# Turning the local probabilities of 26 of 32 head pairs on VectorE instead of TensorE

## The chip, the cores and the metric

The kernel runs on one core of a Trainium2 chip. The metric is device time in microseconds. The kernel before took 578.76 us, the median of three runs (578.58 to 580.44).

A core has five engines that each work through an instruction list of their own, in order: TensorE (PE in the profile; its weight loads are PEld), VectorE (DVE), ScalarE (ACT), GpSimd (POOL) and SyncE (SP, which here issues nearly all DMAs). They wait for each other through semaphores.

## The reference

For 8 batches, 8 heads, a sequence of 576 and a head size of 64, the output of an attention with two resolutions goes through a gated MLP:

```python
# per batch and head
out_d   = softmax(scale * q_d @ k_d.T) @ v_d      # q, k, v averaged over 4 positions: 144 x 144
mask    = abs(i - j) < 4                          # 7 diagonals of the 576 x 576 scores
out_loc = softmax(where(mask, scale * q @ k.T, -1e9)) @ v
x = repeat(out_d, 4) + out_loc                    # heads side by side: 576 x 512 per batch
# per batch
h = gelu_tanh(x @ w_in);  u, v = halves of h      # 512 -> 1024
v_n = layernorm(v) * g;   v_s = w_sg @ v_n + b_sg # mixes the 576 positions
y = x + (u * v_s) @ w_out
```

All of it is float32. The matrix products of the MLP are made of three products of a high and a low part each, which is why they fill most of TensorE's time.

## The kernel before

**Pairs.** Two heads make a pair of 128 partitions, and pairs are numbered 0 to 31 (`g`), four per batch. The local attention never builds the 576 x 576 scores. The queries are cut into ten blocks of 58 (`QB`), and the keys that a block can see lie in a window of 64 (`KB`), so a pair's local scores are ten tiles of 64 queries by 64 keys for each of two heads. The tile `ms` holds them as 128 partitions x 10 x 64: partitions 0 to 63 are queries of one head, 64 to 127 of the other. Within a window, query j sees keys j to j+6, so all else in the 64 x 64 tile is zero after the exponential.

**Steps of a pair,** by the names of its tasks: `lq lk lv lw` load; `qs ks vs` pool over four positions; `YS` makes both kinds of scores on TensorE; `ma mb` add the mask (L463); `mx nx my ny` find the maxima; `ea eb ec` take exponentials on ScalarE (L515, L523); `re rc` sums and reciprocals; `np` (L537) normalises the local probabilities in `ms`, on GpSimd or VectorE; `nq` (L540) the pooled ones. Then both are turned, since the product with `v` needs keys on the partitions: `T` (four transposes through TensorE, L543, each 122 queries x 128 keys, into a PSUM bank), `U` (a fifth of these, and three of the pooled ones, L552) and `t` (two pooled). `pa` and `pb` copy the local results from PSUM into a buffer `pt` (helper `copy`, L232), on ScalarE or VectorE; `pc pe` do so for the pooled ones. `D` (L604, L620) multiplies with `v` on TensorE, and `oe od xa xb xh xl xc` merge, store in `x` and split it into a high and low part.

**MLP of a batch:** `v u s o` on TensorE (L722 and L800) and, between them, work on the other engines: `vg vb vp vn vh vl ua sa sm gh gl oa os`.

**Order.** Every engine's list follows one text, `ORDER`, that names all tasks, with the engine behind a slash where it isn't the first that the task allows (`np23/V`: VectorE). It was written by a planner beforehand; at build time `place()` only walks it. So where a task stands in `ORDER` decides what stands in front of it and behind it on its engine. The dictionaries in `add(...)`, such as `{"A": 0.52, "V": 0.58}`, are the planner's costs in us, and have no effect on what is built.

**Buffers.** `place()` also hands out buffers, first freed first used: 8 PSUM banks (`ps`), 10 large buffers (`X`) and 38 of `R`. A task that takes a buffer waits for the last readers of what was in it. `ms` is an `X`; `pt`, `pdt`, the loaded `q k v` and most of the MLP's operands are `R`.

Of the kernel before, what the change touches and what calls it, by code (L numbers as in the profile page):

```python
# [112 lines left out]
YS9 lq11 nq8/P od7 xa7 xb7 xh7/A T8 ma9 my9 mb9 mx9 ny9/A ec9 U8 nx9/V ea9 t8 pa8/V pb8/V qs11/V ks10/V xl6/P pc8/A
pe8/V xl7/P os0.0 v1.0 vg1.0 vb1.0 v1.1 vg1.1 lv8 vs8 D8 oe8/A od8 YS10 my10 eb9 xa8 xb8 xc6 lv9 xc7 vb1.1 ma10 re9/V
v1.4 va1.4/A mb10 xh8/A vs9 vp1.1 vn1.1 v1.3 rc9 nq9/V lk12 vg1.3 v1.2 vp1.0 np9/P t9 T9 vj1.4 vn1.0 U9 o0.2 vg1.4 lw9
lk11 vg1.2 ks12/P pa9/A pb9/A pc9/A lq12 ks11/P ny10/A mx10 nx10/A ec10 vb1.3 vp1.3 vn1.3 vh1.3/A vl1.3/P pe9/V
vh1.1/V u1.2 vb1.2 vp1.2 ea10 oa0.2 oa0.3 D9 YS11 vb1.4 my11 vh1.0/V vl1.0/P eb10 ny11/V ma11 mb11 oe9/V re10/A u1.1
rc10 np10/V vl1.1/V nq10/P ec11 u1.4 ua1.4 ua1.2 u1.0 ua1.0 os0.3 vp1.4 ua1.1 mx11 vn1.2 vh1.2/V vl1.2/P T10 pa10/A
vn1.4 lv10 vh1.4/A vl1.4/V vs10 t10 U10 pb10/V u1.3 ua1.3 pc10/V pe10/A lq13 nx11/A ea11 s1.3 qs12/V eb11 xl8/V od9
xa9 s1.0 s1.1 sa1.1 sa1.0 sm1.1/V lk13 re11/A rc11 lw10 D10 YS12 oe10/A lv11 vs11 xb9 sa1.3 xh9/A np11/P sm1.0/P  # L120
nq11/P u1.6 lw11 lq14 qs13/P my12 ny12/A ma12 s1.2 mb12 mx12 ec12 nx12/V ea12 od10 xa10 s1.5 eb12 sa1.2 ua1.6 s1.4
xl9/P T11 xc8 os0.2 pa11/A sm1.3/V sm1.2/P gh1.1/A re12/V rc12 t11 np12/V sa1.5 nq12/P sa1.4 U11 pb11/V pc11/V u1.5
xb10 pe11/A ua1.5 sm1.5/P ks13/V t12 D11 YS13 lv12 oe11/A od11 xa11 lk15 xb11 ma13 T12 pa12/A U12 pb12/A xh10/A s1.6
mb13 pc12/V pe12/A my13 ny13/V ec13 mx13 nx13/V s1.7 lk14 ks14/V u1.7 xl10/V xh11/V xl11/V sm1.4/P v2.0 u2.6 ks15/P
eb13 vs12 qs14/P sa1.6 ea13 re13/V ua2.6 rc13 ua1.7 vg2.0 v2.3 os0.1 np13/P T13 pa13/A gh1.0/V gl1.0/P lw12 sm1.6/V
D12 lv13 oe12/A sa1.7 sm1.7/V gh1.3/V gl1.3/V gl1.1/V YS14 nq13/P U13 od12 xa12 gh1.2/A lw13 t13 vg2.3 vb2.0 xc11 ma14
mb14 gl1.2/P lq15 o1.4 my14 pb13/V xb12 ny14/V vs13 mx14 v2.1 ec14 lq16 o1.0 pc13/V nx14/A vp2.0 vn2.0 vh2.0/V pe13/V
D13 oa1.4 ea14 qs15/V eb14 oa1.0 YS15 my15 re14/V ny15/V ec15 ma15 mb15 mx15 rc14 v2.2 vg2.2 lk16 xc10 xc9 v2.4 lv14
vg2.1 vs14 np14/V vb2.1 T14 lw14 va2.4/A vj2.4 nx15/A nq14/P vl2.0/V oe13/A od13 xa13 xb13 ks16/P vp2.1 qs16/V vn2.1
vh2.1/A pa14/A lq17 U14 pb14/V t14 vg2.4 pc14/A pe14/A o1.5 u2.0 oa1.5 os1.2 ua2.0 u2.4 ua2.4 vb2.2 vp2.2 vn2.2  # L130
vh2.2/V xh13/A o1.2 ea15 D14 vb2.4 oe14/A vl2.2/P eb15 vp2.4 re15/A YS16 ma16 u2.1 oa1.2 mb16 o1.6 mx16 nx16/V o1.7
lq18 o1.3 eb16 lk18 vb2.3 my16 vl2.1/P ny16/V vn2.4 vh2.4/A oa1.6 xh12/A ec16 vp2.3 vn2.3 vh2.3/V vl2.3/V vl2.4/P
# [879 lines left out]
```

## Time and profile before

| | |
|---|---|
| runs | 578.76 us median (578.58 to 580.44) |
| profiled execution, span | 578.3 us |
| TensorE busy | 562.3 us, 97% |
| TensorE weight loads busy | 524.0 us, 91% |
| VectorE busy | 420.8 us, 73% |
| ScalarE busy | 355.8 us, 62% |
| GpSimd busy | 309.6 us, 54% |
| mean granted TensorE clock | 0.991 |

The span runs from the first to the last instruction of one profiled execution; it lies 0.5 us under the median of the runs. A busy share is that of the whole span. TensorE's matmuls are pipelined, so the duration of one is longer than the distance to the next; where a cost of TensorE is needed, distances from start to start are read. VectorE's instructions can overlap a little with the next one too. In the profile's rows a group reads: line, engine, operation, output<-inputs, form, count | busy us in total, mean ns of one | idle time of the engine before them, and what ended it.

### The profile page before, as it was taken

Reading aid. Unit: us, or ns where it says so; the run is one execution under the profiler, and the core shown is the slowest. Engines: PE = TensorE matmul, PEld = TensorE weight load, DVE = VectorE, ACT = ScalarE, POOL = GpSimd, SP = SyncE. Lnnn points to the kernel's source line nnn. Section 1 sums busy time; section 2 is a strip of 40 time slices with the busy share of each in tenths; the row PEclk is TensorE's granted clock in tenths of the full one; section 3 lists DMA queues with packets and bytes.
Section 4 is the critical chain, followed back from the end, with each engine's and each line's share of the span. In section 5 each row is a group of like instructions: output and inputs, shape, how many; then the busy total and the mean of one; then the engine's idle time right before and its main releaser. Section 6 shows DMA issues by size and latency. Waiting matters only on the chain.

```text
span 578.3 us, 17588 instructions
## 1 busy us (share of the span) xinstructions
PE 562.3 (97%) x7040; PEld 524.0 (91%) x7040; DVE 420.8 (73%) x943; ACT 355.8 (62%) x1239; POOL 309.6 (54%) x391
## 2 busy tenths in 40 slices
PE   7986999999999999999999999999999999999997
PEld 5775899989998899979999899988999889998997
DVE  7987989878877886677567678878757687553552
ACT  4895996978775794475648596465825678211310
POOL 6685647776875546524567824375266743401330
PEclk9897999999999999999999999999999999999999
DMA  8879214263435031610216413143326330001102
GB/s 310 276 234 313 98 45 120 96 192 87 140 96 164 24 107 54 208 63 1 86 56 197 114 67 98 41 151 98 87 83 195 103 107 2 18 23 41 43 1 102
DMA packets 30609, 62.73 MB, mean 108 GB/s; under 512 B 3648, under 2 KB 3904, under 8 KB 30528
## 3 DMA queue, kind: packets, MB, share of 16 engines
q1 hardware_dynamic: 29952, 60.39, 33.1%
q8 instruction: 55, 0.90, 0.7%
q10 hardware_dynamic: 576, 1.23, 0.6%
q14 instruction: 26, 0.21, 0.1%
HBM read 52.17 MB, written 9.44 MB: 107 GB/s over the span
## 4 chain that ended last, share of the span: by engine, by line
PE 91%; DVE 4%; DMA 2%; ACT 2%; issue 1%; ACTq 0%; DVEq 0%
PE ps L800 55%; PE ps L722 18%; PE ps L604 4%; PE ps L620 3%; PE ps L455 3%; PE ps L543 3%; PE ps L476 3%; PE ps L552 2%; DMA R<-in_qT_dram 1%; PE ps L955 1%; ACT L523 1%; ACT pd L523 1%; DVE stats L485 0%; PE ps L448 0%; DMA R<-in_v_dram 0%
## 5 line engine op out<-in xcount | busy, mean ns | idle before, releaser
L800 PE MATMUL ps<-wsg_h,R 128*128 128x288 f32 x576 | 120.5, 296 | 0.0
L800 PE MATMUL ps<-X,weight_z 128*128 128x288 f32 x512 | 109.4, 297 | 0.0
L800 PE MATMUL ps<-R,weight_r 128*128 128x288 f32 x768 | 108.4, 297 | 1.0 <-ACT R L734 0.8
L800 PEld LDWEIGHTS ps<-R,weight_r 128*128 128x128 f32 x768 | 103.1, 188 | 2.2 <-ACT R L734 0.9
L722 PE MATMUL ps<-weight_y,X 128*128 128x512 f32 x320 | 99.1, 404 | 0.0
L515 ACT ACTIVATE X<-X,nb 128x64 f32<-128x64 f32 x280 | 93.6, 339 | 2.8 <-DVE nb L494 2.3
L800 PEld LDWEIGHTS ps<-wsg_h,R 128*128 128x128 f32 x576 | 94.0, 188 | 0.2 <-DVE R L791 0.2
L800 PE MATMUL ps<-wsg_l,R 128*128 128x288 f32 x320 | 92.5, 295 | 0.0
L800 PEld LDWEIGHTS ps<-X,weight_z 128*128 128x128 f32 x512 | 84.3, 188 | 0.5
L800 PE MATMUL ps<-R,weight_z 128*128 128x288 f32 x256 | 75.5, 295 | 0.0
L722 PEld LDWEIGHTS ps<-weight_y,X 128*128 128x128 f32 x320 | 59.4, 191 | 12.5
L838 DVE SCALAR_TENSOR_TENSOR vs<-ps,g_sb,b_sb 128x288 f32<-128x288 f32 x64 | 32.7, 514 | 49.3 <-PE ps L800 43.9
L232 ACT CAST R<-R 128x512 fp32r<-128x512 f32 (+2 forms) x41 | 26.0, 645 | 62.4 <-DVE R L845 35.2
L800 PEld LDWEIGHTS ps<-wsg_l,R 128*128 128x128 f32 x320 | 60.3, 188 | 0.0
L763 POOL TENSOR_TENSOR rs<-rs,nhalf 128x1 f32<-128x1 f32 (+1 forms) x40 | 25.5, 641 | 64.9 <-DVE rs L754 60.9
L515 ACT ACTIVATION_READ_ACCUMULATOR X<-X,nb 128x1 f32 x280 | 53.5, 191 | 0.0
L722 PE MATMUL ps<-weight_y,R 128*128 128x512 f32 x128 | 51.2, 400 | 0.0
L439 POOL TENSOR_TENSOR pairs<-R 112x256 f32<-112x256 f32 x56 | 44.4, 793 | 9.2 <-DMA R<-in_v_dram 9.2
L845 POOL TENSOR_TENSOR R<-R,vs 128x288 f32<-128x288 f32 x27 | 23.7, 880 | 47.1 <-DVE vs L838 32.0
L800 PEld LDWEIGHTS ps<-R,weight_z 128*128 128x128 f32 x256 | 48.2, 188 | 0.2
L232 ACT COPY R<-ps 112x288 f32<-112x288 f32 (+4 forms) x77 | 30.1, 419 | 27.5 <-PE ps L543 20.0
L791 POOL TENSOR_TENSOR R<-R,R 128x512 fp32r<-128x512 f32 (+1 forms) x22 | 30.6, 1393 | 28.4 <-DVE R L232 6.4
(124 smaller groups left out, 1197.3 us busy)
## 6 DMA issues: line engine op xcount, KB each, us to landing
R<-in_v_dram SPq DMA_DIRECT2D x56, 224.0 KB, 3.8
X<-in_vw_dram SPq DMA_DIRECT2D x31, 320.0 KB, 4.2
R<-in_kT_dram SPq DMA_DIRECT2D x31, 293.0 KB, 4.3
out_dram<-R SPq DMA_DIRECT2D x31, 288.0 KB, 3.0
R<-in_qT_dram SPq DMA_DIRECT2D x30, 293.0 KB, 4.0
weight_y<-in_w_in_dram SPq DMA_DIRECT2D x4, 512.0 KB, 6.0
weight_z<-in_w_in_dram SPq DMA_DIRECT2D x4, 512.0 KB, 6.1
weight_r<-in_w_out_dram SPq DMA_DIRECT2D x4, 512.0 KB, 6.6
```

What stands on the lines that cost most here:

```text
L232: (nc.scalar.copy if e == "A" else ENG[e].tensor_copy)(**kw)
L439: ENG[e].tensor_tensor(out=pairs, in0=v[:, 0:2], in1=v[:, 2:4], op=ALU.add)
L455: nc.tensor.matmul(out=sp[i][os, c * KB:(c + 1) * KB], lhsT=q[hs, t * QB:t * QB + KB], rhs=k[hs, t * QB:t * QB + KB], start=not early, sto ...
L476: nc.tensor.matmul(out=st["sdv"][n][os, cs], lhsT=qd2[par][hs, i * QC:i * QC + HD], rhs=st["kd"][hs, ks], start=True, stop=True)
L515: nc.scalar.activation(out=st["ms"][:, t, :], in_=src, func=AF.Exp, bias=st["nb"][:, t:t + 1], scale=scale, accum_out=sums[par][:, t:t + 1])
L604: nc.tensor.matmul(out=out, lhsT=lhsT, rhs=pdt[ks, probs, h * QC:(h + 1) * QC], start=first, stop=last)
L722: nc.tensor.matmul(out=acc, lhsT=r32(l), rhs=r32(weights[f"y{k}"][:, 0, w]), start=(i == 0 and ks[0] == 0), stop=(i == len(ops) - 1 and ks ...
L763: nc.gpsimd.tensor_tensor(out=rs[0:n], in0=rs[0:n], in1=nhalf[0:n], op=ALU.pow)
L791: ENG[e].tensor_tensor(out=r32(dst), in0=vact[s][0][0:n], in1=vh[0:n, 0:DM], op=ALU.subtract)
L800: nc.tensor.matmul(out=acc[:, 0:HALF], lhsT=r32(l), rhs=r32(r), start=(first and n == 0), stop=(last and n == len(ops) - 1))
L838: nc.vector.scalar_tensor_tensor(out=vsb[i], in0=at["ps", "m", b, "s", i][:, 0:HALF], scalar=g_sb[:, i // 2:i // 2 + 1], in1=b_sb[:, half( ...
L845: ENG[e].tensor_tensor(out=u[:, half(i)], in0=u[:, half(i)], in1=vsb[i], op=ALU.mult)
```

## The change

From pair 6 on (`FLIP = 6`), the local probabilities don't pass through TensorE. Twelve VectorE instructions per pair write them turned, straight from `ms` into one of two kept buffers `pz` (pool `Z`), which are zeroed once on GpSimd (`hz0`, `hz1`). Each instruction turns a strip of five 32 x 32 squares (32 partitions x 160 elements in, the same out), one square from each of five of the ten tiles. Of the four squares of a 64 x 64 tile the one with queries 32 to 63 and keys 0 to 31 is always zero and is left alone, so three squares for each of two heads (`a`) and two tile parities (`i`) make twelve.

`T`, `pa` and `pb` are gone for these pairs, and `U` keeps only its three pooled transposes. The four tasks `h{g}.0` to `h{g}.3`, three instructions each, stand in `ORDER` where `T{g}` stood. `R` shrinks from 38 to 35 buffers. A few loads (`lq17 lk17 lq18 lk18 lk24 lq28 lv30`) stand later, `os2.0` and two high parts (`vh5.1 vh5.3`) moved by a few places; else the order is as before.

```diff
+SQ = 32
...
-SIZES = {"ps": 8, "X": 10, "R": 38}
+SIZES = {"ps": 8, "X": 10, "R": 35, "Z": 2}
+FLIP = 6
...
+    pz = [const.tile([P, NTP, 2, KB], F32, name=f"pz{i}") for i in range(SIZES["Z"])]
...
+    for i, t in enumerate(pz):
+        add(f"hz{i}", {"P": 0.6}, lambda e, t=t: nc.gpsimd.memset(t, 0.0))
...
+        def flips(a, i):
+            def emit(e):
+                st["pt"] = pz[where["Z", "pt", g]]
+                src = st["ms"].rearrange("p (c i) k -> p c i k", i=2)[:, :, i]
+                for qb, kb in ((0, 0), (0, 1), (1, 1)):
+                    qs, ks, k0 = a * KB + qb * SQ, slice(kb * SQ, (kb + 1) * SQ), i * KB + kb * SQ
+                    nc.vector.transpose(out=st["pt"][k0:k0 + SQ, :, a, qb * SQ:(qb + 1) * SQ], in_=src[qs:qs + SQ, :, ks])
+            return emit
...
         def turn2(e):
             t2 = buf("ps", "t", g, 2)
-            turn_pair(t2[:, 0:LD], 4)
+            if not flip:
+                turn_pair(t2[:, 0:LD], 4)
...
-            v, pt = st["vw"], st["pt"].rearrange("p c (a q) -> p c a q", a=2)
+            v, pt = st["vw"], st["pt"] if flip else st["pt"].rearrange("p c (a q) -> p c a q", a=2)
...
-                                         rhs=pt[ks, c, h ^ int(2 * c + i >= NA)], start=True, stop=True)
+                                         rhs=pt[ks, c, h ^ int(2 * c + i >= NA), 0:QB], start=True, stop=True)
...
+        if flip:
+            flipped = [f"h{g}.{i}" for i in range(4)]
+            for n, (a, i) in enumerate(((0, 0), (0, 1), (1, 0), (1, 1))):
+                add(flipped[n], {"V": 0.7}, flips(a, i), [N("np")] + (flipped[:1] if n else []),
+                    takes=[] if n else [("Z", "pt", g)], gives=[("X", "ms", g)])
+        else:
+            flipped = [N("pa"), N("pb")]
...
         add(N("D"), {"T": 2.8 if early_d else 1.0}, av,
-            [N("pa"), N("pb"), N("lw"), N("pc"), N("pe"), N("D", 2), N("lv" if early_d else "vs")],
+            flipped + [N("lw"), N("pc"), N("pe"), N("D", 2), N("lv" if early_d else "vs")],
```

An excerpt of `ORDER` around pair 23, before and after:

```diff
-re23/A rc23 nq23/V ks24/V np23/V vg4.3 vb4.3 o3.5 oa3.5 u4.6 ua4.6 ua4.4 ua4.3 vl4.0/P lw22 D22 vp4.3 vn4.3 lw23
-oe22/V YS24 oa3.0 oa3.1 lq26 vh4.3/V T23 pa23/A u4.5 ua4.5 ma24 mb24 mx24 nx24/V eb24 vh4.4/V vl4.4/V vl4.3/P s4.0
+re23/A rc23 nq23/V np23/V o3.5 lk24 ks24/V vg4.3
+vb4.3 oa3.5 u4.6 ua4.6 ua4.4 ua4.3 vl4.0/P lw22 D22 vp4.3 vn4.3 lw23 oe22/V YS24 oa3.0 oa3.1 lq26 vh4.3/V h23.0
+h23.1 h23.2 h23.3 u4.5 ua4.5 ma24 mb24 mx24 nx24/V eb24 vh4.4/V vl4.4/V vl4.3/P s4.0
```

More of the change, by code (lines that the diff above doesn't have):

```diff
@@ L113 @@
[L113 to L132, printed above, removed]
@@ new lines @@
+re8/A o0.4 ks9/V oa0.4 xc5 t7 np7/P h7.0 h7.1 h7.2 h7.3 oa0.0 oa0.5 vs7 U7 pc7/A xc4 rc8 oa0.1 np8/P o0.3 pe7/V D7
+oe7/V xh6/A YS9 lq11 nq8/P od7 xa7 xb7 xh7/A h8.0 h8.1 h8.2 h8.3 ma9 my9 mb9 mx9 ny9/A ec9 U8 nx9/V ea9 t8 qs11/V
+ks10/V xl6/P pc8/A pe8/V xl7/P os0.0 v1.0 vg1.0 vb1.0 v1.1 vg1.1 lv8 vs8 D8 oe8/A od8 YS10 my10 eb9 xa8 xb8 xc6 lv9
+xc7 vb1.1 ma10 re9/V v1.4 va1.4/A mb10 xh8/A vs9 vp1.1 vn1.1 v1.3 rc9 nq9/V lk12 vg1.3 v1.2 vp1.0 np9/P t9 h9.0 h9.1
+h9.2 h9.3 vj1.4 vn1.0 U9 o0.2 vg1.4 lw9 lk11 vg1.2 ks12/P pc9/A lq12 ks11/P ny10/A mx10 nx10/A ec10 vb1.3 vp1.3 vn1.3
@@ new lines @@
+vh1.3/A vl1.3/P pe9/V vh1.1/V u1.2 vb1.2 vp1.2 ea10 oa0.2 oa0.3 D9 YS11 vb1.4 my11 vh1.0/V vl1.0/P eb10 ny11/V ma11
+mb11 oe9/V re10/A u1.1 rc10 np10/V vl1.1/V nq10/P ec11 u1.4 ua1.4 ua1.2 u1.0 ua1.0 os0.3 vp1.4 ua1.1 mx11 vn1.2
+vh1.2/V vl1.2/P h10.0 h10.1 h10.2 h10.3 vn1.4 lv10 vh1.4/A vl1.4/V vs10 t10 U10 u1.3 ua1.3 pc10/V pe10/A lq13 nx11/A
+ea11 s1.3 qs12/V eb11 xl8/V od9 xa9 s1.0 s1.1 sa1.1 sa1.0 sm1.1/V lk13 re11/A rc11 lw10 D10 YS12 oe10/A lv11 vs11 xb9
+sa1.3 xh9/A np11/P sm1.0/P nq11/P u1.6 lw11 lq14 qs13/P my12 ny12/A ma12 s1.2 mb12 mx12 ec12 nx12/V ea12 od10 xa10
@@ new lines @@
+u2.1 oa1.2 mb16 o1.6 mx16 nx16/V o1.7 o1.3 eb16 vb2.3 my16 vl2.1/P ny16/V vn2.4 vh2.4/A oa1.6 xh12/A ec16 vp2.3 vn2.3
+vh2.3/V vl2.3/V lk18 vl2.4/P ua2.1 s2.4 lw15 od14 xa14 oa1.7 oa1.3 o1.1 lq18 lq17 xl13/V qs18/P lk17 xb14 u2.2 s2.0
+sa2.0 rc15 oa1.1 s2.2 nq15/V s2.1 ea16 np15/V s2.3 sa2.1 u2.3 xl12/P lv15 re16/A vs15 sm2.0/V sa2.2 sm2.1/P s2.6 h15.0
+h15.1 h15.2 h15.3 ua2.2 rc16 nq16/P np16/V h16.0 h16.1 h16.2 h16.3 gh2.0/A gl2.0/P xc13 ks17/V U15 os1.0 t15 sa2.3
+ua2.3 sm2.3/V sm2.2/V sa2.4 s2.5 gh2.1/A xh14/V gl2.1/P sm2.4/P qs17/P u2.5 sa2.5 u2.7 pc15/V pe15/A ua2.5 sa2.6
@@ new lines @@
+np21/V vg4.2 v4.4 va4.4/A U20 h21.0 h21.1 h21.2 h21.3 vb4.2 vg4.1 vb4.1 h20.0 h20.1 h20.2 h20.3 vj4.4 t20 pc20/V
+pe20/A lk23 ks23/V v4.0 vg4.0 D20 vp4.2 oe20/V YS22 ma22 mb22 t21 U21 pc21/V pe21/A mx22 lv21 my22 ny22/V ec22 nx22/A
+qs23/P ea22 vb4.0 u4.2 od20 xa20 xb20 eb22 re22/A o3.2 oa3.2 vs21 lq24 D21 lv22 YS23 ma23 mb23 my23 mx23 vp4.1 vn4.1
+vh4.1/A vs22 lk25 ny23/V ec23 vn4.2 oe21/V od21 xa21 rc22 u4.3 nq22/P nx23/V u4.0 ua4.0 o3.0 ua4.2 qs24/V u4.1 t22
+vh4.2/A np22/V h22.0 h22.1 h22.2 h22.3 U22 ua4.1 vl4.2/P os2.3 pc22/A pe22/A vp4.0 vn4.0 v4.3 xb21 vg4.4 vb4.4 ks25/V
@@ new lines @@
+xh21/V vp4.4 vl4.1/P eb23 u4.4 vh4.0/V vn4.4 o3.3 oa3.3 o3.1 ea23 re23/A rc23 nq23/V np23/V o3.5 lk24 ks24/V vg4.3
+vb4.3 oa3.5 u4.6 ua4.6 ua4.4 ua4.3 vl4.0/P lw22 D22 vp4.3 vn4.3 lw23 oe22/V YS24 oa3.0 oa3.1 lq26 vh4.3/V h23.0 h23.1
+h23.2 h23.3 u4.5 ua4.5 ma24 mb24 mx24 nx24/V eb24 vh4.4/V vl4.4/V vl4.3/P s4.0 sa4.0 sm4.0/V lv23 s4.2 lw24 vs23
+xl21/V ea24 s4.1 qs26/V sa4.2 sa4.1 sm4.1/P s4.3 my24 ny24/V sa4.3 U23 ec24 t23 s4.5 u4.7 sm4.2/P sm4.3/V gh4.0/V
+gh4.1/V gl4.1/V gl4.0/V lq25 xh20/A od22 qs25/V re24/A rc24 nq24/P np24/V xa22 sa4.5 pc23/V pe23/A sm4.5/P xb22 s4.4
@@ new lines @@
+ec26 u5.0 u5.4 vn5.2 v5.3 vg5.3 xb24 vs25 pe25/V ua5.0 vn5.1 xh24/A vh5.2/V D25 lv26 vs26 YS27 ma27 lq29 vp5.0 mb27
+oe25/A my27 u5.2 ua5.2 ua5.4 mx27 lw27 qs29/P o4.1 vl5.2/P ny27/A vn5.0 vh5.0/A os2.0 vl5.0/P eb26 u5.5 od25 xa25 xb25
+vb5.3 vp5.3 vn5.3 o4.0 oa4.0 vb5.4 vp5.4 vn5.4 o4.5 ea26 re26/V ec27 o4.3 oa4.3 o4.4 lq28 vh5.1/A vh5.3/A lk29 u5.3
+rc26 nx27/A vl5.1/V eb27 lk28 vh5.4/V vl5.3/V vl5.4/V s5.5 s5.0 nq26/V sa5.0 sm5.0/P np26/V s5.2 s5.1 sa5.2 sm5.2/P
+xl24/P ea27 lw26 re27/A qs28/P u5.1 oa4.4 ua5.3 s5.3 ua5.1 oa4.5 os4.3 sa5.1 s5.4 oa4.1 sm5.1/V sa5.3 xh25/A rc27
@@ L681, in attention @@
         add(N("nq"), {"P": 0.98, "V": 0.5}, norm_d, [N("rc")])
-        add(N("T"), {"T": 0.44}, turn, [N("np")], takes=[("ps", "t", g, 1)], gives=[("X", "ms", g)])
-        add(N("U"), {"T": 0.42}, turn2, [N("np"), N("nq")], takes=[("ps", "t", g, 2)], gives=[("X", "ms", g)])
+        if flip:
[5 more added lines that the diff above has]
+            flipped = [N("pa"), N("pb")]
+            add(N("T"), {"T": 0.44}, turn, [N("np")], takes=[("ps", "t", g, 1)], gives=[("X", "ms", g)])
+            add(N("pa"), {"A": 0.52, "V": 0.58}, evac(0, 4, 1), [N("T")], takes=[("R", "pt", g)], gives=[("ps", "t", g, 1)])
+            add(N("pb"), {"A": 0.18, "V": 0.19}, evac(4, 1, 2), [N("U"), N("pa")])
@@ L684, in attention @@
+        add(N("U"), {"T": 0.42}, turn2, ([] if flip else [N("np")]) + [N("nq")], takes=[("ps", "t", g, 2)],
+            gives=[] if flip else [("X", "ms", g)])
         add(N("t"), {"T": 0.31}, turn3, [N("nq")], takes=[("ps", "t", g, 3)])
-        add(N("pa"), {"A": 0.52, "V": 0.58}, evac(0, 4, 1), [N("T")], takes=[("R", "pt", g)], gives=[("ps", "t", g, 1)])
-        add(N("pb"), {"A": 0.18, "V": 0.19}, evac(4, 1, 2), [N("U"), N("pa")])
-        add(N("pc"), {"A": 0.35, "V": 0.44}, evac_d(0, 3, 2, LD), [N("U"), N("pb")], takes=[("R", "pdt", g)], gives=[("ps", "t", g, 2)])
+        add(N("pc"), {"A": 0.35, "V": 0.44}, evac_d(0, 3, 2, LD), [N("U")] + ([] if flip else [N("pb")]), takes=[("R", "pdt", g)], gives=[("ps", "t", g, 2)])
```

131 lines of the change are left out of this document (62 added, 69 removed).

## The prediction

> **What bounds the kernel now.** I read the page's busy times and its chain of work first, then the list of waits, then busy times by stage.
>
> ```profile
> span 578.3 us, 17588 instructions
> PE 562.3 (97%) x7040; PEld 524.0 (91%) x7040; DVE 420.8 (73%) x943; ACT 355.8 (62%) x1239; POOL 309.6 (54%) x391
> PE 91%; DVE 4%; DMA 2%; ACT 2%; issue 1%; ACTq 0%; DVEq 0%
> ```
>
> TensorE is busy 97% of the span and makes up 91% of the chain that ends last. It hardly waits for anyone; in the list of waits (who <- for whom: us in total, times, longest) these are its longest and the only one of the transposes:
>
> ```profile
> PE ps L620 <- issue: 4.5, 1, 4.5
> ...
> PE ps L543 <- DVE X L537: 0.4, 1, 0.4
> ```
>
> So work taken off TensorE is time saved, as long as the other engines keep up. Which is next shows by stage. I cut the stretch from 94 us, when the probabilities of pair 6 are normalised, to 508 us, when the last pair is multiplied with `v`. Columns: stretch, its length, then for each engine busy us (instructions), TensorE's clock, DMA share, GB/s.
>
> ```profile
> 94.00:160.00 66.00, 65.61 (x1027) 61.12 (x1026) 55.84 (x129) 53.06 (x200) 47.03 (x60) 1.00 0.43 131
> 160.00:230.00 70.00, 70.00 (x874) 66.43 (x873) 53.57 (x122) 48.55 (x169) 39.92 (x51) 1.00 0.30 91
> 230.00:300.00 70.00, 68.71 (x766) 64.61 (x765) 47.86 (x107) 41.35 (x125) 33.91 (x44) 1.00 0.25 78
> 300.00:360.00 60.00, 60.00 (x886) 55.81 (x885) 45.25 (x105) 41.65 (x152) 37.01 (x48) 1.00 0.41 123
> 360.00:430.00 70.00, 70.00 (x778) 66.55 (x776) 51.31 (x114) 39.87 (x143) 32.52 (x43) 1.00 0.30 96
> 430.00:508.00 78.00, 77.71 (x1000) 73.51 (x1001) 55.45 (x126) 47.24 (x158) 42.29 (x57) 1.00 0.26 79
> ```
>
> TensorE (first pair of figures) is full in each. VectorE (third) has 10 to 25 us left in each, and that is the room for the change. How full VectorE can get while TensorE loses nothing shows in a denser stretch: 46.81 of 50 us, 94%, with TensorE at 49.61.
>
> ```profile
> 60.00:110.00 50.00, 49.61 (x640) 47.37 (x639) 46.81 (x93) 44.11 (x137) 31.30 (x32) 1.00 0.28 87
> ```
>
> **What it removes.** Five transposes per pair from TensorE. The timeline around 198 us (start, duration, engine, line, operation) shows one pair's five, then its pooled ones:
>
> ```profile
> 198.26 0.69 PE L543 MATMUL ps<-turn_l,X 122*128 122x122 f32 x5
> ...
> 198.78 0.64 PE L552 MATMUL ps<-turn_p,pd 112*112 112x112 f32 x5
> ```
>
> From start to start five take 198.78 - 198.26 = 0.52 us. The 26 pairs have 130 of them, so TensorE loses 26 x 0.52 = 13.5 us of work.
>
> The copies `pa` and `pb` go too. Their groups, with those of the first six pairs:
>
> ```profile
> L232 DVE COPY R<-ps 128x464 f32<-128x464 f32 x9 | 5.7, 634 | 3.7 <-PE ps L543 3.7
> L232 DVE COPY R<-ps 128x116 f32<-128x116 f32 x19 | 5.1, 266 | 0.7 <-PE ps L552 0.6
> L232 ACT COPY R<-ps 128x464 f32<-128x464 f32 x23 | 12.5, 548 | 20.0 <-PE ps L543 20.0
> ```
>
> In the order, 8 of the 9 and 16 of the 19 on VectorE belong to pairs 6 to 31: 8 x 0.634 + 16 x 0.266 = 9.3 us. Successive VectorE instructions overlap by about 0.09 us (below), so some 7.2 us of VectorE's time come free, 0.28 per pair. What ScalarE gains is worth nothing here: it is at most 80% busy in the stages above and is not what TensorE waits for.
>
> **What it adds: 12 strips per pair on VectorE.** The trace has no such instruction, so I bound it. Each strip has 160 elements per partition; only 32 partitions take part, but that doesn't help, since 64 partitions take as long as 128 (L791 below has both, with a minimum of 676 and a median of 689 ns). Rows of SBUF-to-SBUF work: two-input instructions (and GpSimd's own `np`, for later), a reduction, ns min/median/max; then plain copies, mean ns.
>
> ```profile
> L791 DVE TENSOR_TENSOR R<-R,R x18: 676/689/1411, 76.2 to 543.8; 128x512 fp32r<-128x512 f32 x12, 64x512 fp32r<-64x512 f32 x6
> ...
> L537 DVE TENSOR_TENSOR X<-X,rc x18: 811/826/1373, 68.3 to 489.1; 128x640 f32<-128x640 f32 x18
> L537 POOL TENSOR_TENSOR X<-X,rc x14: 1259/1272/1679, 19.6 to 469.0; 128x640 f32<-128x640 f32 x14
> ...
> L422 DVE TENSOR_REDUCE kd<-R x17: 734/742/747, 21.6 to 387.8; 128x144 f32<-128x576 f32 x17
> ...
> L303 DVE COPY turn_p<-ident_sb 112x48 f32<-112x48 f32 x4 | 0.5, 183 | 0.0
> L303 DVE COPY turn_l<-ident_sb 122x6 f32<-122x6 f32 x1 | 0.2, 165 | 0.0
> ```
>
> From 512 to 640 elements the time grows by 137 ns, 1.07 ns per element, with 141 ns fixed: 312 ns for 160. From 6 to 48 copied elements it grows by 0.43 ns each: 231 ns for 160. A strip has one input like the copy, but it must reorder, and the reduction, which has one input and isn't a copy either, fits the slower line (141 + 576 x 1.07 = 757 against 742). I take 312.
>
> The second question is how far strips overlap. In this stretch of the timeline each row starts before the one ahead of it ends, except around the instruction that writes partitions 64 to 127 while it reads 0 to 63 (`vl1.4`, L791):
>
> ```profile
> 146.66 0.43 DVE L232 CAST R<-R 128x512 fp32r<-128x512 f32 x1
> 147.01 0.53 DVE L771 TENSOR_SCALAR R<-R,mv,rs 64x512 f32<-64x512 f32 x1
> 148.23 1.00 DVE L791 TENSOR_TENSOR R<-R,R 64x512 fp32r<-64x512 f32 x1 [0.69 <-ACT R L232]
> 149.26 0.64 DVE L232 COPY R<-ps 128x116 f32<-128x116 f32 x2
> ```
>
> L771 starts 0.08 us before L232 has ended. The copies at 149.26 use nothing of L791's, yet start 0.03 after its end. Another place shows the same for a read that begins at another partition (the copy at 473.92 reads from partition 64 and starts 0.03 after L771's end):
>
> ```profile
> 473.35 0.54 DVE L771 TENSOR_SCALAR R<-R,mv,rs 128x512 f32<-128x512 f32 x1
> 473.92 0.69 DVE L232 COPY R<-ps 64x512 f32<-64x512 f32 x1
> ```
>
> So where the first partition changes, instructions don't overlap, which costs about 0.12 us each. Of a pair's twelve strips every one differs from the one before it in the quarter it reads from or the one it writes to (for one `a` and `i`: read 0, 0, 1; write 0, 1, 1). Each then costs 0.312 + 0.03 = 0.34 us, a pair 4.1. The Trainium skill, "VectorE: DVE Perf Modes", section "Two Vector instructions with no wait between them", calls such an instruction held, for a changed start quadrant of input or output; by the output alone 8 of 12 strips would be held and a pair would cost 8 x 0.34 + 4 x 0.22 = 3.6 us, by the whole rule 4.1, and the trace agrees on both sides with its gaps of +0.03. The same page's table in "The three transpose paths" gives 311 ns for 128 columns of bf16; an estimate from it, with 32 columns more at 1.04 ns, is 345 ns, and a pair would cost 4.5 us.
>
> The bounds: overlapping, 0.312 - 0.09 = 0.22 us and 2.7 per pair; overlapping and at the copies' rate, 0.231 - 0.09 = 0.14 and 1.7; upwards, not overlapping and slowed as L791's 64-partition form is on average (763 against its median of 689, 11%), 0.38 and 4.5. I take 4.1, which the change of partitions points to, so 3.8 net of the copies.
>
> **The sum.** The transposes of L543 count the pairs of a stage, five each; the same windows with that line alone:
>
> ```profile
> 94.00:160.00 66.00, 3.92 (x25) 2.85 (x25) 1.00 0.43 131
> ...
> 430.00:508.00 78.00, 4.52 (x30) 3.42 (x30) 1.00 0.26 79
> ```
>
> The counts are 25, 20, 25, 19, 11 and 30, so 5, 4, 5, 4, 2 and 6 pairs. Per stage, VectorE's need is its busy time plus 3.8 per pair: 74.8, 68.8, 66.9, 60.5, 58.9, 78.3 us. TensorE's need is the length less 0.52 per pair: 63.4, 67.9, 67.4, 57.9, 69.0, 74.9. VectorE now needs more in four of six stages, and about as much in a fifth. Both lists are in order and `D` waits for the strips, so a stage lasts about as long as the longer of TensorE's need and VectorE's divided by how full it can be. I take 95%, a little over the 94% seen where it was not the bound: 78.8, 72.4, 70.4, 63.6, 69.0, 82.4, in all 436.6 for 414, +22.6 us. At 100% it would be +4.8, at 90% +43. The span becomes 578.3 + 22.6 = 600.9, and with the 0.5 us between span and median, 601.
>
> **The other edits.** The strips stand where `T` stood; behind them on VectorE are the next pair's masks and the MLP's PSUM copies (L838, L874), whose banks TensorE needs; that is how lateness comes back. For nine pairs GpSimd does `np`, and the strips of 9, 13 and 28 come so soon behind it that VectorE waits for up to GpSimd's 1.27 us each; that is in the 5%. Zeroing costs GpSimd two passes over 640 elements near 55 us, where it is busy 5.52 of 10 us (the 50 to 60 us row below): nothing; without that cover at most 2 x 1.27 = 2.5, as `np` has as many elements. Fewer `R` buffers make seven loads later. The worst is `lk24`: it gets a buffer that `o3.5` frees, and `ks24` on VectorE stands right behind it.
>
> ```profile
> 350.22 0.75 DVE L422 TENSOR_REDUCE kd<-R 128x144 f32<-128x576 f32 x1
> 351.42 0.29 PE L800 MATMUL ps<-X,weight_z 128*128 128x288 f32 x1
> R<-in_kT_dram SPq DMA_DIRECT2D x31, 293.0 KB, 4.3
> ```
>
> `ks24` ran at 350.22, while `o3.5` ended as the next product began, at 351.42. With 4.3 us for the load VectorE, if on time, would wait until 355.8; a VectorE that is late by as much waits for nothing. It costs 0 to 4.3 us; by the forecast VectorE is late there, and I count it in the 5% too. `lq18` does the same to GpSimd, which is 57% busy there (39.92 of 70); the other five have more work between load and use. All nothing; without that slack 4.3 us each.
>
> **Rivals.** (1) The strips overlap after all (2.7 per pair, 2.4 net): VectorE needs, at 95%, 71.4, 66.5, 63.0, 57.7, 59.1, 73.5; only the first stage is bound by it, the sum is 408.5, 5.5 less, and the time 573. For it: most VectorE neighbours in the trace overlap. Against: the rows with a change of partitions. The wait for `lk24` would take up to 4.3 of the 5.5 us back. (2) They also run at the copies' rate (1.7, 1.4 net): only the first stage is longer than TensorE's need, 66.1 for 63.4, and 13.5 - 2.7 = 10.8 us are saved: 568. For it: a strip has one input in SBUF, as the L303 copies. (3) Worse than the forecast: TensorE's clock falls. These windows show the 4.5 us pause of the waits above (L620, it begins at 45.6) and what follows it:
>
> ```profile
> 40.00:50.00 10.00, 4.87 (x182) 4.49 (x173) 6.45 (x15) 9.86 (x37) 7.13 (x7) 0.95 0.97 293
> 50.00:60.00 10.00, 9.94 (x50) 8.04 (x50) 8.46 (x15) 3.33 (x14) 5.52 (x6) 0.71 1.03 332
> ```
>
> The clock in the ten us behind it is 0.71: 2.9 us lost. If each of four crowded stages had one such pause, that is 12 us more, 613. Against: new pauses are likely shorter than 4.5 us each, spread over 26 pairs.
>
> **Chances.** Forecast 0.66 (0.01 of it within 0.3%), rival 1 0.16 (faster 0.10, within 0.04, slower 0.02), rival 2 0.09, rival 3 0.09. A difference under 0.3%, 1.7 us, can't be told from none. Faster 0.19, within 0.05, slower 0.76. The range: below it lies rival 2; above, strips at 4.5 with VectorE 90% full give 85.4, 78.2, 76.5, 68.9, 69.0 and 89.6, +53.6, 632. I take 571 to 632; the forecast's own is 584 (100% full) to 632.
>
> **What would show it.** Right: strips of 0.31 to 0.35 us that start 0.03 after each other; VectorE 93% busy or more from 94 to 360 us; TensorE's waits, now near none, 30 us or more there, ended by the strips and by L463, L838 and L874. Wrong: strips that overlap or take under 0.25 us, VectorE at 90% or less with TensorE still full; or VectorE saturated and the time unchanged, because idle time I count as forced isn't.

## The result: 17% slower, more than four times the loss that was forecast

| | before | after |
|---|---|---|
| runs, median | 579.60 us (578.58 to 580.47) | 680.14 us (679.32 to 681.73) |
| ratio, 95% interval | 1 | 1.1735 [1.1711, 1.1759] |
| profiled execution, span | 578.3 us | 677.8 us |
| TensorE busy | 562.3 us, 97% | 583.3 us, 86% |
| VectorE busy | 420.8 us, 73% | 520.9 us, 77% |
| mean granted TensorE clock | 0.991 | 0.94 |

The direction was right. The loss was not 22 us but 100, and the time lies 48 us above the upper end of the range.

The page of the kernel after, with its chain of work by engine and by line:

```profile
span 677.8 us, 17606 instructions
PE 583.3 (86%) x6910; PEld 536.1 (79%) x6910; DVE 520.9 (77%) x1231; ACT 344.9 (51%) x1211; POOL 306.7 (45%) x393
PE 36%; DVE 24%; ACT 5%; issue 4%; POOL 3%; DMA 1%; ACTq 0%; DVEq 0%; POOLq 0%
PE ps L825 25%; DVE pz L568 10%; PE ps L747 6%; ACT X L522 3%; DVE R L235 1%; PE ps L637 1%; PE ps L621 1%; DVE X L544 1%; DVE vs L863 1%; DVE st L777 1%; PE ps L462 1%; DVE R L870 1%; DVE R L644 1%; PE ps L483 1%; PE ps L559 1%
```

VectorE has 100.1 us more to do, and the span is 99.5 us longer. Its idle time over the span is 157.5 us before (578.3 - 420.8) and 156.9 after (677.8 - 520.9): **in sum, none of the idle time that the forecast counted on was used.** The chain of work that was 91% TensorE now passes from engine to engine, with TensorE at 36% and VectorE at 24%; the strips alone (L568) make up 10% of the span on it.

The same for the stretch with the pairs 6 to 31, from 94 us on: first the kernel before, then the kernel after (busy us of TensorE, weight loads, VectorE, ScalarE, GpSimd, each with its instructions; clock; DMA share; GB/s).

```profile
94.00:508.00 414.00, 412.02 (x5321) 388.05 (x5322) 309.28 (x698) 271.73 (x943) 232.67 (x299) 1.00 0.32 98
```

```profile
94.00:600.00 506.00, 425.91 (x5063) 392.69 (x5062) 403.57 (x973) 258.03 (x909) 223.92 (x292) 0.93 0.26 81
```

Before, TensorE idles for 2.0 us of 414 and VectorE for 104.7. After, TensorE idles for 80.1 us of 506 and VectorE for 102.4. VectorE is 80% busy, TensorE 84%: neither is full.

The strips themselves, from the view of their line (minimum, median and maximum ns, then the idle time before them and who waited for them):

```profile
L568 DVE STREAM_TRANSPOSE pz<-X x312: 322/336/343, 97.3 to 594.5; 32x160 f32<-32x160 f32 x156
its engine sat idle before it (us, times) until:
  POOL X L544: 2.6, 2
who waited for it (us, times):
```

The last list is empty: the trace puts no engine's wait down to a strip. What TensorE waits for stands behind the strips on VectorE. Its longest waits in the kernel after (who <- for whom: us, times, longest):

```profile
PE ps L621 <- DVE R L235: 16.3, 5, 7.4
PE ps L825 <- DVE R L816: 10.7, 5, 4.4
PE ps L621 <- ACT R L235: 10.1, 3, 4.4
PE ps L559 <- DVE pd L547: 8.9, 2, 5.7
PE ps L825 <- DVE R L882: 8.7, 2, 7.6
```

L235 is the copy helper (L232 before), L621 the product of the pooled probabilities with `v`, L825 the MLP's products (L800 before), L816 the low parts `vl`, L547 `nq` and L882 the low parts `gl` (L857 before). And where VectorE idles, before and after:

```profile
DVE vs L838 <- PE ps L800: 43.9, 29, 5.0
DVE R L874 <- PE ps L800: 19.3, 15, 4.3
```

```profile
DVE vs L863 <- PE ps L825: 35.9, 24, 5.0
DVE R L899 <- PE ps L825: 22.6, 15, 4.3
```

These are waits for the MLP's products: `sa` (L838, then L863) and `oa` (L874, then L899). They are the two largest parts of VectorE's idle time, 63.2 of 157.5 us before. They belong to certain places in VectorE's list, and the places of the strips are others.

### The profile page after: what moved, and what is told of

It is laid out like the page before. It is cut to its first block, busy times and chain, and to the rows that moved or that the text cites. A ratio compares the mean times of both kernels' runs of the same rounds, so it can differ in the third digit from the quotient of the medians.

```text
span 677.8 us, 17606 instructions
## 1 busy us (share of the span) xinstructions
PE 583.3 (86%) x6910; PEld 536.1 (79%) x6910; DVE 520.9 (77%) x1231; ACT 344.9 (51%) x1211; POOL 306.7 (45%) x393
## 3 DMA queue, kind: packets, MB, share of 16 engines
q10 hardware_dynamic: 576, 1.23, 0.5%
## 4 chain that ended last, share of the span: by engine, by line
PE 36%; DVE 24%; ACT 5%; issue 4%; POOL 3%; DMA 1%; ACTq 0%; DVEq 0%; POOLq 0%
PE ps L825 25%; DVE pz L568 10%; PE ps L747 6%; ACT X L522 3%; DVE R L235 1%; PE ps L637 1%; PE ps L621 1%; DVE X L544 1%; DVE vs L863 1%; DVE st L777 1%; PE ps L462 1%; DVE R L870 1%; DVE R L644 1%; PE ps L483 1%; PE ps L559 1%
## 5 line engine op out<-in xcount | busy, mean ns | idle before, releaser
L825 PE MATMUL ps<-wsg_h,R 128*128 128x288 f32 x576 | 128.1, 309 | 12.6 <-DVE R L816 10.7
L825 PE MATMUL ps<-R,weight_r 128*128 128x288 f32 x768 | 113.2, 304 | 9.9 <-DVE R L882 8.7
L825 PE MATMUL ps<-X,weight_z 128*128 128x288 f32 x512 | 111.4, 301 | 6.3 <-DVE vs L863 3.0
L825 PEld LDWEIGHTS ps<-R,weight_r 128*128 128x128 f32 x768 | 107.0, 194 | 12.0 <-DVE R L882 9.1
L825 PEld LDWEIGHTS ps<-wsg_h,R 128*128 128x128 f32 x576 | 100.0, 200 | 14.2 <-DVE R L816 11.9
L568 DVE STREAM_TRANSPOSE pz<-X 32x160 f32<-32x160 f32 x312 | 104.7, 336 | 6.7 <-POOL X L544 2.6
L825 PE MATMUL ps<-wsg_l,R 128*128 128x288 f32 x320 | 96.4, 306 | 0.0
L825 PEld LDWEIGHTS ps<-X,weight_z 128*128 128x128 f32 x512 | 85.5, 190 | 7.7 <-DVE vs L863 3.3
L825 PE MATMUL ps<-R,weight_z 128*128 128x288 f32 x256 | 76.2, 298 | 0.0
L235 ACT CAST R<-R 128x512 fp32r<-128x512 f32 (+2 forms) x41 | 26.0, 645 | 97.7 <-DVE R L870 53.7
L825 PEld LDWEIGHTS ps<-wsg_l,R 128*128 128x128 f32 x320 | 63.9, 200 | 0.0
L863 DVE SCALAR_TENSOR_TENSOR vs<-ps,g_sb,b_sb 128x288 f32<-128x288 f32 x64 | 32.6, 513 | 40.2 <-PE ps L825 35.9
L825 PEld LDWEIGHTS ps<-R,weight_z 128*128 128x128 f32 x256 | 48.9, 191 | 0.2
L621 PE MATMUL ps<-R,vd 48*64 48x144 f32 (+1 forms) x448 | 22.2, 295 | 27.3 <-DVE R L235 15.5
L899 DVE TENSOR_TENSOR R<-ps,R 128x288 f32<-128x288 f32 x64 | 27.6, 447 | 22.6 <-PE ps L825 22.6
```

What stands on the lines that cost most here:

```text
L235: (nc.scalar.copy if e == "A" else ENG[e].tensor_copy)(**kw)
L568: nc.vector.transpose(out=st["pt"][k0:k0 + SQ, :, a, qb * SQ:(qb + 1) * SQ], in_=src[qs:qs + SQ, :, ks])
L621: nc.tensor.matmul(out=out, lhsT=lhsT, rhs=pdt[ks, probs, h * QC:(h + 1) * QC], start=first, stop=last)
L825: nc.tensor.matmul(out=acc[:, 0:HALF], lhsT=r32(l), rhs=r32(r), start=(first and n == 0), stop=(last and n == len(ops) - 1))
L863: nc.vector.scalar_tensor_tensor(out=vsb[i], in0=at["ps", "m", b, "s", i][:, 0:HALF], scalar=g_sb[:, i // 2:i // 2 + 1], in1=b_sb[:, half( ...
L899: nc.vector.tensor_tensor(out=x[:, half(i)], in0=at["ps", "m", b, "o", i][:, 0:HALF], in1=x[:, half(i)], op=ALU.add)
```

## The experiments

The theory after the result: VectorE's idle time can't be used by a block that stands at another place in its list, so on average nearly every microsecond of strips goes into the time. Its rivals: the edits beside the strips cost it; the block of twelve is the fault, and spreading helps; the fallen clock costs it; the strips slow VectorE's other instructions.

**The edits beside the strips alone.** The order of the kernel after with `T`, `pa` and `pb` put back, the copies writing into the two kept buffers, `R` still 35, no strips:

```diff
+STRIPS = ()
-        early, early_d, flip = g < EARLY_S, g < EARLY_D, g >= FLIP
+        early, early_d, flip, kept = g < EARLY_S, g < EARLY_D, g in STRIPS, g >= FLIP
-                copy(e, out=st["pt"][:, c0:c0 + n], in_=src)
+                    copy(e, out=st["pt"][:, c0:c0 + n, :, 0:QB], in_=src.rearrange("p c (a q) -> p c a q", a=2))
```

> The changed kernel's order of loads, its 35 R buffers and the two kept buffers, but the local probabilities still turned by T and copied by pa and pb, now into the kept buffers. No strips. If the strips themselves cost the 100 us, this takes 577 to 582 us, as the kernel before. If the fewer buffers and the later loads carry a large part of it (GpSimd waits up to 8.7 us for v in the changed kernel's profile), it takes 590 us or more.

Measured: 586.23 us, ratio 1.0128 [1.0104, 1.0151], between the two forecasts. So 7.5 us of the 100 are not the strips'. VectorE's timeline of this kernel at `ks24` (start, duration, operation, idle time before it and what ended it):

```profile
350.52 0.82 DVE L543 TENSOR_TENSOR X<-X,rc 128x640 f32<-128x640 f32 x1
353.32 0.76 DVE L428 TENSOR_REDUCE kd<-R 128x144 f32<-128x576 f32 x1 [1.98 <-DMA R<-in_kT_dram]
```

The load `lk24` came late, by the mechanism that the prediction named, for 1.98 of the 4.3 us it allowed. Reading the start of each pair's local product (L620, part of `D`) in this trace against the kernel before, nothing is lost up to pair 18 (1.5 us ahead); then it is 0.9 us ahead at pair 19, 0.3 late at 20, 2.2 at 23, 3.7 at 24 and 6.2 at 26, and hardly more after that. So the loss falls between pairs 18 and 26. What takes the part that isn't `lk24`'s wasn't tried.

**TensorE's side alone.** No strips and no transposes either; `pz` stays zero, so the local product multiplies zeros and the local part of the output is left out:

```diff
-                for qb, kb in ((0, 0), (0, 1), (1, 1)):
+                for qb, kb in ():
```

> TensorE's side of the change alone: pairs 6 to 31 have no T, pa and pb and no strips either, so their local product multiplies the zeros in the kept buffers and the local part of the output is left out. The sum of the prediction: 578.8 - 13.5 = 565 us (563 to 567). If TensorE's saving is not worth its 0.52 us per pair, 570 us or more.

Measured: 578.95 us, runs from 575.4 to 581.8, ratio 0.9999 [0.9973, 1.0024]. Against the first experiment this is 7.3 us less, for 13.5 us of work taken off TensorE. (By the profiled spans, 573.6 and 584.6, it is 11.0, but that of 573.6 belongs to the fastest of this kernel's ten runs.) The 565 us that the sum gave for this side were not reached. The rest of the way, from 578.95 to 680.14, is the strips: 101.2 us. They take 26 x 4.19 = 109 us of VectorE (4.19 is a block of twelve in the timelines below), so 93% of their duration appears in the time.

That is a mean over pairs. Comparing the starts of the local products in the two traces, the kernel after loses 8.7 us between the products of pairs 15 and 16, with one block of strips between them in the order, and nothing between those of 21 and 22 or of 27 and 28, also with one block each. The strips don't slow VectorE's other instructions as a whole: it is busy for 416.5 us here and for 520.9 in the kernel after, 104.4 more, and the 312 strips alone take 104.7.

**Every second pair.** Strips for 13 pairs, `T` and copies for the others:

```diff
+STRIPS = range(FLIP, NB * NPAIR, 2)
```

> Pairs 6, 8, ... 30 (13 of 26) are turned by strips, the others as in e1. Theory of fullness, the prediction's own with VectorE 95% full at most: VectorE then has room in five of six stages and TensorE sets the time, 572 to 580 us. Theory of place: VectorE isn't full, but each block of 12 strips holds up the work that stands behind it on VectorE, and TensorE runs ahead by less than a block; then each pair costs its 3.9 us whatever the others do, and half of them give half, about 629 us.

Measured: 637.21 us, 1.1005 [1.0964, 1.1045], 8 us over the forecast by place and far from that by fullness. From 586.23 that is 51.0 us for half the pairs, where all of them take 93.9. VectorE has room in plenty on average and the cost is there all the same:

```profile
PE 575.0 (91%) x6975; PEld 527.9 (83%) x6975; DVE 476.6 (75%) x1086; ACT 350.8 (55%) x1226; POOL 309.4 (49%) x393
```

The prediction's sum by stages has a threshold, VectorE's being nearly full, below which strips cost nothing. Here VectorE is 75% busy and 51 us are lost.

**Half the strips of each pair.** Six instead of twelve, so half of the local probabilities is missing in the product:

```diff
-                for qb, kb in ((0, 0), (0, 1), (1, 1)):
+                for qb, kb in ((0, 0), (0, 1), (1, 1))[:2 - a]:
```

> The changed kernel with 6 of the 12 strips in each block; the others' part of the local probabilities stays zero, so part of the local output is left out. The kernel without strips (e4) took 579, the whole one 680. If TensorE runs ahead of VectorE by a time that a block must exceed before it costs anything, half a block costs less than half, 600 to 620 us; if each us costs the same from the first, 630 us.

Measured: 618.39 us, 1.0695 [1.0646, 1.0744]. Six strips per pair cost 39.4 us over the kernel without any, the other six 61.8. Per pair that is 1.5 us for 2.1 us of strips, then 2.4 us for another 2.1. So a part of a block is hidden, and the rest is paid. How large that part is can't be read from the mean: the second six cost more than their own duration, and the trace with six has three stretches of 6.83 us at half the clock (from 195.1, 270.2 and 352.1 us) that the kernel without strips hasn't; they can have lost 3.4 us each, at most 10.2 of the 39.4.

**Place against place.** Six pairs (15, 19, 23, 26, 30, 31) alone, once as blocks at `T`'s place, once with the same 72 strips as single instructions ahead of VectorE instructions that had waited for TensorE or a load (for pair 19, nine ahead of `sa3.0` and three ahead of `sa3.1`):

```diff
+STRIPS = (15, 19, 23, 26, 30, 31,)
 # blocks                            # in gaps
-vh3.3/A h19.0 h19.1 h19.2 h19.3 ea18 oa2.1 u3.2
+vh3.3/A ea18 oa2.1 u3.2 ... vl3.3/P s3.0 h19.0 ... h19.8 sa3.0 ... s3.1 h19.9 h19.10 h19.11 sa3.1
```

> As e1 (586 us), but six pairs (15, 19, 23, 26, 30, 31) are turned by strips, in blocks at T's place as in the changed kernel. In the changed kernel these six pairs' multiplications came 5.4, 0, 10.9, 5.9, 2.4 and 0 us later than the pair before them did, less what the buffers cost. If every us added to VectorE costs a us wherever it stands, 6 x 3.9 more: 609 us. If it is the place, the sum of those steps: about 600 to 610 us.

> The same six pairs and the same 72 strips as e5, but each strip stands directly ahead of a VectorE instruction that sat waiting for TensorE or a load for 0.3 us or more in e1's trace, as many as fit into the wait. If VectorE's waiting time can be used, the strips cost nothing and TensorE is spared six times 0.52 us: 582 to 587 us. If lateness of VectorE costs a us per us wherever it stands (e3 speaks for that), 609 us as e5.

Measured: 605.52 us as blocks, 1.0477 [1.0445, 1.051]; 586.56 in the gaps, 1.0131 [1.0096, 1.0167]. Against the 586.23 without strips the blocks cost 19.3 us, 3.2 per pair, and the same strips in the gaps 0.3, which is within the noise. VectorE's work is the same to 0.4 us, but its idle time isn't: 159.1 us of the span without strips, 159.6 with blocks, 142.6 in the gaps. Blocks, then gaps:

```profile
PE 568.6 (94%) x7010; PEld 525.9 (87%) x7010; DVE 444.4 (74%) x1012; ACT 352.7 (58%) x1230; POOL 309.6 (51%) x393
```

```profile
PE 563.1 (96%) x7010; PEld 522.3 (89%) x7010; DVE 444.0 (76%) x1012; ACT 352.9 (60%) x1230; POOL 310.7 (53%) x393
```

VectorE's timeline at pair 19, as blocks first:

```profile
283.16 4.17 DVE L567 STREAM_TRANSPOSE pz<-X 32x160 f32<-32x160 f32 x12
...
290.11 0.52 DVE L868 SCALAR_TENSOR_TENSOR vs<-ps,g_sb,b_sb 128x288 f32<-128x288 f32 x1 [1.69 <-PE ps L830]
290.54 0.74 DVE L428 TENSOR_REDUCE qd<-R 128x144 f32<-128x576 f32 x1
293.54 0.52 DVE L868 SCALAR_TENSOR_TENSOR vs<-ps,g_sb,b_sb 128x288 f32<-128x288 f32 x1 [2.25 <-PE ps L830]
```

and in the gaps:

```profile
284.02 3.12 DVE L570 STREAM_TRANSPOSE pz<-X 32x160 f32<-32x160 f32 x9
287.53 0.52 DVE L871 SCALAR_TENSOR_TENSOR vs<-ps,g_sb,b_sb 128x288 f32<-128x288 f32 x1 [0.39 <-PE ps L833]
287.97 0.74 DVE L431 TENSOR_REDUCE qd<-R 128x144 f32<-128x576 f32 x1
288.72 1.04 DVE L570 STREAM_TRANSPOSE pz<-X 32x160 f32<-32x160 f32 x3
291.00 0.52 DVE L871 SCALAR_TENSOR_TENSOR vs<-ps,g_sb,b_sb 128x288 f32<-128x288 f32 x1 [1.23 <-PE ps L833]
```

Without strips (the first experiment) the same two instructions wait like this:

```profile
284.81 0.52 DVE L868 SCALAR_TENSOR_TENSOR vs<-ps,g_sb,b_sb 128x288 f32<-128x288 f32 x1 [3.14 <-PE ps L830]
288.27 0.52 DVE L868 SCALAR_TENSOR_TENSOR vs<-ps,g_sb,b_sb 128x288 f32<-128x288 f32 x1 [2.28 <-PE ps L830]
```

As a block the strips run first, and VectorE then still waits 1.69 of the 3.14 us and 2.25 of the 2.28. In the gaps they take the place of the waits, of which 0.39 and 1.23 us are left. By the starts of the local products in these traces against the first experiment's, the block of pair 19 costs 1.3 us, that of 15 costs 3.4, that of 23 costs 6.5, that of 26 2.2, and those of 30 and 31 together 5.8. How a block is paid for shows most plainly at pair 23: the block, the low part `vl` (L821) behind it on VectorE, the product of TensorE that waits for `vl`, and TensorE's clock around it (0.83 in the third column from the end):

```profile
363.00 4.18 DVE L567 STREAM_TRANSPOSE pz<-X 32x160 f32<-32x160 f32 x12
369.51 0.68 DVE L821 TENSOR_TENSOR R<-R,R 64x512 fp32r<-64x512 f32 x1
370.25 0.61 PE L830 MATMUL ps<-wsg_h,R 128*128 128x288 f32 x1 [4.37 <-DVE R L821]
360.00:380.00 20.00, 14.90 (x168) 14.37 (x160) 14.83 (x39) 6.64 (x29) 5.69 (x8) 0.83 0.16 51
```

The list of VectorE's waits says the same over the whole kernel, 37.9 us for `sa` with blocks and 22.0 in the gaps:

```profile
DVE vs L868 <- PE ps L830: 37.9, 26, 5.4
```

```profile
DVE vs L871 <- PE ps L833: 22.0, 21, 5.0
```

So for these six pairs **the place decides, not the load**. A part of the difference is the clock, as a consequence: the trace with blocks has two stretches of 6.83 us at half the clock, behind the pauses near pairs 23 and 30, which the one with gaps hasn't. Of the 17.4 us between the two spans TensorE idles 11.9 and is busy 5.5 us longer. Whether fillers would return that here wasn't tried. The 6 x 0.52 = 3.1 us taken off TensorE hardly show: the median in the gaps is that without strips, and in the trace the local products gain 1.0 us from pair 14 to pair 31.

**Spreading the strips.** Twelve tasks of one strip, spread evenly over VectorE's instructions between `T`'s place and `D`, and in a second kernel over the first 60% of that way:

```diff
-                for qb, kb in ((0, 0), (0, 1), (1, 1)):
+                for qb, kb in (sq,):
-            flipped = [f"h{g}.{i}" for i in range(4)]
+            flipped = [f"h{g}.{i}" for i in range(12)]
```

> The changed kernel, but a pair's 12 strips are single tasks, spread evenly over VectorE's list from the place of the block to the pair's multiplication D; their number and sizes are the same. Theory of fullness: no less time, about 680 us, as VectorE has as much to do. Theory of place: no task waits behind more than one or two strips, so most of the 100 us go: 590 to 630 us.

> As e3, but the 12 strips are spread over the first 60% of VectorE's list between the place of the block and D, so that D doesn't wait for the last strips (in e3 it did, 32 us in all). If place decides, the waits of e3 on the strips go and nothing comes instead: 630 to 650 us. If the cost is VectorE's time wherever it stands, 670 to 680 us.

Measured: 676.17 us, 1.1677 [1.1637, 1.1717], and 665.47 us, 1.1509 [1.1449, 1.157]. The theory of place, in the form it had here, missed both times: the first lies near the forecast by fullness, the second between the two. The first is confounded: its last strips are so late that `D` waits for them, which no instruction did in the block form (L654 is `D`'s local product, L579 the strip):

```profile
PE ps L654 <- DVE pz L579: 32.0, 19, 3.9
```

In the second this wait falls to 0.3 us, and another comes in its place: the product of the pooled probabilities, also part of `D`, waits for VectorE's copies (L246):

```profile
PE ps L638 <- DVE R L246: 23.4, 12, 6.1
```

So spreading gains only 14.7 us of 101. An explanation is that most pairs have no gaps within reach. Counted in the trace of the kernel with copies and no strips (VectorE's waits of 0.3 us or more between the end of `np` and the start of the local product, 0.349 us per strip), 21 of the 26 pairs have room for fewer than twelve strips, pairs 6 and 7 for none, pair 30 for 26 and pair 19 for 33. That place and not VectorE's load sets the cost is shown for the six pairs above; whether any order would hide the strips of the others was not tried.

**The clock.** Fillers on TensorE, 630 small matmuls ahead of 30 tasks that had waited, so that it doesn't go idle:

```diff
-WARM = {"S0": 28, "S3": 20}
+WARM = {"S0": 28, "S3": 20, "o0.7": 64, "D7": 31, "D8": 10, "u1.2": 10, ... "D29": 26, "u6.2": 11}
```

> The changed kernel, with TensorE kept busy where it stood still: ahead of each of the 30 tasks in front of or in which its profile has TensorE idle for 0.6 us or more (67 us after fill at 0.9, as in 12 to 64 matmuls of zeros of 0.107 us each) fillers are issued into the bank that the task takes anyway. In the changed kernel 15 pieces of 3.4 to 10 us, 82.5 us in all, ran at half clock, and TensorE's busy time rose to 583 where 549 was due, 34 us. If that is lost on the path, the clock goes back to 0.99 and the time to 645 to 655 us. If VectorE sets the pace and TensorE only waits less long when it is slow, it stays at 675 to 685 us.

Measured: 674.93 us, 1.166 [1.1617, 1.1703], clock 0.984. Its row for the stretch from 94 us:

```profile
94.00:600.00 506.00, 477.25 (x5705) 431.83 (x5704) 401.93 (x978) 259.96 (x912) 223.30 (x292) 0.99 0.26 81
```

The clock is back at 0.99, TensorE is 94% busy with the fillers, and VectorE does 401.93 us of work in the same 506 as without them (403.57). The time falls by 5.2 us. A filler can also be in the way of a product that could start, so the clock's own share isn't settled to the microsecond. But with the clock nearly back, 95 us of the loss are still there.

**TensorE's saving beside the strips.** Five transposes per pair kept on TensorE although the strips do the work:

```diff
-            for c in range(4):
+            for c in (0, 1, 2, 3, 3) if flip else range(4):
+            add(N("T"), {"T": 0.55}, turn, [N("np")], takes=[("ps", "t", g, 1)], gives=[("ps", "t", g, 1), ("X", "ms", g)])
```

> The changed kernel, with the five transposes per pair left on TensorE beside the strips (26 x 0.52 = 13.5 us), their result unread. If the 13.5 us taken off TensorE still count in the changed kernel, 693 us; if TensorE's waits for VectorE swallow them, 680 us.

Measured: 676.87 us, 1.1703 [1.1642, 1.1764], not distinguishable from 680.14. In the changed kernel no gain shows from the 13.5 us that the change takes off TensorE.

## Why the prediction was right in direction and wrong in size

**What bounds the kernel before: right.** TensorE was the bound, and work taken off it alone is time saved, though 7.3 us of 13.5 by the medians.

**The price of a strip: right.** 336 ns at the median where 312 were taken, and no overlap: a block of twelve takes 4.18 to 4.19 us, 0.349 per strip, where the sum had 0.34 and 4.1 per pair (the prediction's other estimate, 345 ns, is nearer still). Here is one on VectorE in the kernel after:

```profile
205.78 0.24 DVE L541 RECIPROCAL rc<-sums 128x13 f32<-128x13 f32 x1
207.46 4.19 DVE L568 STREAM_TRANSPOSE pz<-X 32x160 f32<-32x160 f32 x12 [1.44 <-POOL X L544]
211.68 0.46 DVE L235 CAST R<-R 128x576 fp32r<-128x576 f32 x1
```

The rivals 1 (they overlap) and 2 (at the copies' rate) fall with it. The 1.44 us before it are GpSimd's `np`, a wait that the prediction named (for pairs 9, 13 and 28; in all 2.6 us, by the view of the line above). The Trainium skill, "VectorE: DVE Perf Modes", section "Two Vector instructions with no wait between them", holds back an instruction whose start quadrant changes. This trace agrees: the twelve last longer than 12 x 0.336 = 4.03 us.

**The step that failed: "I take 95%".** The sum gave each stage the longer of TensorE's need and VectorE's need divided by how full VectorE can be. VectorE's needs came to 408.2 us in all (74.8 + 68.8 + 66.9 + 60.5 + 58.9 + 78.3), and 403.57 were measured: that was right too. The divisor was wrong. The measured share is 403.57 / 506 = 0.80, in place of 0.95. (That share is the outcome, and no constant that one could have put into the sum.) The 94% from 60 to 110 us showed that VectorE *can* be that full when its list fits TensorE's. They did not show that work put at another place is taken up by its idle time. The largest parts of that idle time were waits for TensorE's products at fixed places in an in-order list (the 43.9 and 19.3 us above). Work put ahead of such waits, with nothing between that TensorE needs soon, was free (0.3 us for 72 strips). Put elsewhere, it delays the operands of the next product (4.37 us at pair 23), TensorE delivers later, and most of the wait comes back (1.69 of 3.14 and 2.25 of 2.28 us at pair 19). A stage of 60 to 78 us holds several such rounds, and a sum by stages doesn't see them.

So the direction came out right partly by luck. The sum had a loss only because VectorE came out nearly full in four stages of six; for half of the pairs the same reasoning gave 572 to 580 us, no loss, and 637 came.

The Trainium skill, "Perfetto Trace Analysis", section "Identifying the Most-Contended Engine", reads VectorE's busy share as a fair measure of how near it is to its limit. Taken as room for more work, that would leave 23% of VectorE in the kernel after. This case doesn't bear that reading out: with VectorE 75% busy (every second pair) and 77% (all of them), what it was given went into the time nearly in full.

**The other edits, put at nothing, with `lk24` in the 5%: too low.** They cost 7.5 us when alone, and a wait of 1.98 us at `ks24` is part of that. The late VectorE that was to hide it is not there in that experiment, so what they cost beside the strips isn't known. The zeroing ran at 39 us and not near 55, in two times 0.63 us.

**Rival 3, the falling clock: it fell, and restoring it returned little.** The clock went from 0.991 to 0.94, in 15 stretches of 3.41 to 10.24 us at half the clock, one of which, near 48 us, the kernel before has too. The rival had four. Its 12 us would have been added to a path that was 91% TensorE, and in the kernel after that share is 36%. With the clock nearly restored 5.2 us came back.

**What was to show it.** Strips of 0.31 to 0.35 us: there. VectorE at 93% or more from 94 to 360 us: not there, 81% (214.90 of 266 us). TensorE's waits of 30 us or more there: there, 48.7 us of idle time (217.35 of 266 busy), but none put down to the strips, and mostly by other lines than those named. The list of what would prove it wrong had "VectorE at 90% or less with TensorE still full". What came was a case that the list lacked: both below 85%, each waiting for the other in turn.

## What to carry to other kernels

Idle time of an engine that works through a list in order is room only at the places where it idles. Before moving work to it, list its waits one by one, and ask at each pair (or tile) whether the work fits ahead of a wait that lies between its input and its use; if not, count the work at about its full duration: here 93% of it on average, though from one pair to the next it was anything from nothing to twice that. An average, even by stages, says nothing of it, and a window in which the engine was nearly full shows only that it can be when the orders match.
